# Attention block for 2048 tokens on one core: x transposed on its way from DRAM, constant query rows written by VectorE

## The chip, the cores and the metric

The kernel runs on one core of a Trainium2 chip. The metric is the device time of one execution in microseconds, the median of several runs of the same program.

## What is computed

A whole multi-head attention block in bfloat16, with one batch, S = 2048 tokens, D = 448 features and 16 heads of 28 features:

```python
qkv = (x @ wqkv).reshape(B, S, 3, H, Dh).transpose(2, 0, 3, 1, 4)
q, k, v = qkv[0], qkv[1], qkv[2]
scores = jnp.einsum("bhqd,bhkd->bhqk", q, k) * (Dh ** -0.5)
p = softmax(scores, axis=-1)
o = jnp.einsum("bhqk,bhkd->bhqd", p, v)
return o.transpose(0, 2, 1, 3).reshape(B, S, D) @ wo
```

## The kernel before

**Tiling.** The 16 heads are worked on in four groups of four (G = 4, HG = 4); each head has a slot of 32 partitions, 28 of them features, so that four heads fill 128 partitions. Queries come in four blocks of 512 (NQC), keys in 16 tiles of 128. A "set" is one group with one query block; there are 16 sets. For each set the scores of a key tile against 512 queries are made on TensorE (L730), turned into exponentials by ScalarE (L928, two half steps of 512 in one pass) or by an approximation in integer arithmetic on VectorE (L943, then L1014 or a GpSimd fill at L979 and an accumulating DMA at L990 for its further terms), and multiplied with V into the bank `o` (L1073). Each score carries a bound in place of the row maximum: it is added through extra rows of the query tile `QP`, which stand beside the 28 features of each head. Some of these rows are constant (the value OFFS), one row per query block holds the bound `su`.

**The beginning.** x is loaded by eight DMAs (`load_x`, L138) in four blocks of 512 rows, each as 128 partitions with 4 rows of 448 (row `16 p + t` of x lies on partition `p`, L133), half of them issued by SP and half by ScalarE's queue. After blocks 0 and 1 come the key and query weights of head group 0 (`load_w0`, L142, into `WG`), and behind x, on SP, all weights of V, Q and K (`load_w`, L135, three DMAs). TensorE transposes each block in pieces of 128 rows by 112 columns (`xt_job`, L613: 16 transposes a block at L621), and ScalarE (L629) and VectorE (L627) copy the results to `XT`, so that features lie on 112 partitions in four chunks. While nothing has landed TensorE runs ten matmuls on zeros to warm up (L643).

`k_first` (L376) then makes the keys of group 0 for each block `sc`: 16 matmuls with `WG[1]` (L298, `mm_proj`), a square of the result on ScalarE (L324), an evacuation to `KA` on VectorE (L393) or ScalarE (L390), a matmul with `blockK` that sums the squares (L409) and a maximum over them on VectorE (L414). After the last block the maximum of all four (L418) and a root by bits (L420) follow. `q_job` makes the first query block (`z`, L457), `qn_first` (L484) its norms and the bound: `nq` (L491), then `su` (L496), which needs the maximum over all keys. With `su` there the first scores can be made. `rows_first` (L658) and `place` (L499) bring `z` and `su` into the tile `QP` by DMAs on SP; until they have landed (`wide`, L734) every score is made by two matmuls, one with `z` and one with `su`.

The constant rows of the 16 tiles `QP` are made by 16 VectorE memsets to zero (L194), followed by 16 small DMAs on SP (L198) that bring OFFS into two partitions each. GpSimd fills constants in the meantime: the identity (L166), the clear of V and its column of ones (L209, L210), the output weights (L216, L219).

**What sets the order.** The kernel has no loops at run time and the compiler does not reorder it. A planner in Python (L234 to L1291) keeps a clock for each engine, a list of jobs (`add`) with an assumed duration, the events that each needs (`need`) and gives, the PSUM bank that it takes (`acq`) and a priority (`pri`, the lowest goes first), and emits instructions in the order of that plan. Each engine then runs its own instructions strictly in this order. The landing times of the first loads are assumed (L637): x's blocks at 4.9, 6.2, 8.0 and 9.3 us, group 0's weights at 6.9, the other weights at 10.9 (V), 12.0 (Q) and 13.2 (K). Two rules of the plan matter here: the banks `a0`, `a1`, `d0`, `d1`, `o` and `m` are handed from job to job, and while nothing else is ready, TensorE gets fillers on zeros (`dense`, L758).

Of the kernel before, what the change touches and what calls it, by code (L numbers as in the profile page):

```python
# [39 lines left out]
def kernel(  # L40
# [7 lines left out]
    nc = tc.nc  # L48
# [5 lines left out]
    G = 4  # L54
    HG = 4
    CC = 4
    CK = D // CC
    QW = 512
    NQC = S // QW
    NKT = S // P  # L60
# [35 lines left out]

    x2 = x[0]
    out2 = out[0]
    out_perm = out2.rearrange("(p t) d -> p t d", t=NKT)

    const = ctx.enter_context(tc.tile_pool(name="const", bufs=1))
    big = ctx.enter_context(tc.tile_pool(name="big", bufs=1))
# [1 line left out]
    wk = ctx.enter_context(tc.tile_pool(name="wk", bufs=2))  # L104
    dram = ctx.enter_context(tc.tile_pool(name="dram", bufs=2, space=bass.MemoryType.DRAM))

    XT = [[big.tile([CK, CC // 2, QW], BF16, name=f"XT{b}_{k}") for k in range(2)] for b in range(NXB)]
    WRAW = [big.tile([CK, CC, D + WPAD], BF16, name=f"WRAW{t}") for t in range(3)]
    WG = [wk.tile([P, QW], F32, name=nm, bufs=n)[0:CK, 0:CC * (HG * Dh + WPAD) // 2].bitcast(BF16)
          .rearrange("p (c n) -> p c n", c=CC) for nm, n in (("rr", 1), ("o_sb", 2))]  # L110
# [2 lines left out]
    for k in range(NTERM):  # L113
# [4 lines left out]
        for b in range(NXB):  # L118
# [4 lines left out]
    xs = [big.tile([P, XB, D], BF16, name=f"xs{b}") for b in range(NXB)]  # L123
    QP = [[[big.tile([P, QW], BF16, name=f"QP{c}_{k}_{z}") for z in range(2)] for k in range(2)] for c in range(NQC)]
    OTL = [big.tile([P, QW], BF16, name=f"OTL{c}") for c in range(NQC)]

    def otile(g, c):
        if g < G - 1:
            return xs[c][:].rearrange("p t d -> p (t d)")[:, g * QW:(g + 1) * QW]
        return OTL[c][:]  # L130

    wq3 = wqkv.rearrange("(cc p) n -> p cc n", p=CK)
    x3 = x2.rearrange("(p t) c -> p t c", t=NKT)  # L133

    def load_w(t, eng):  # L135
        eng.dma_start(out=WRAW[t][:, :, 0:D], in_=wq3[:, :, t * D:(t + 1) * D])

    def load_x(b, eng, k=0, n=1):  # L138
        w = XB // n
        eng.dma_start(out=xs[b][:, k * w:(k + 1) * w, :], in_=x3[:, b * XB + k * w:b * XB + (k + 1) * w, :])  # L140

    def load_w0(t, eng):  # L142
        eng.dma_start(out=WG[t], in_=wq3[:, :, t * D:t * D + HG * Dh + WPAD])

    load_x(0, nc.sync, 0, 2)
    load_x(0, nc.scalar, 1, 2)
    for b in range(1, NXB):
        load_x(b, nc.sync, 0, 2)
        load_x(b, nc.scalar, 1, 2)
        if b == 1:  # L150
            load_w0(1, nc.sync)
            load_w0(0, nc.scalar)
    load_w(2, nc.sync)
    load_w(0, nc.sync)
    load_w(1, nc.sync)

    from concourse.hw_specs import get_activation_tables
    for idx, funcs in enumerate(get_activation_tables(nc.m.arch, ()).values()):
# [3 lines left out]
            break  # L162


    ident = const.tile([P, P], BF16, name="ident")
    nc.gpsimd.memset(ident[:], 0.0)  # L166
    nc.gpsimd.affine_select(out=ident[:], in_=ident[:], compare_op=ALU.not_equal,
# [9 lines left out]
    offs = wk.tile([P, 2 * QW], BF16, name="pt", bufs=NPT)[0:2, 0:QW]  # L177
# [4 lines left out]
    for i in range(HG):  # L182
# [4 lines left out]
        nc.vector.memset(blockK[rows, HP * i:HP * (i + 1)], MARG4)  # L187
        for c in range(NQC):
            nc.vector.memset(maskK[rows, c, HP * i + Dh + c:HP * i + Dh + c + 1], 1.0)
    nc.vector.memset(offs, OFFS)  # L190
    for c in range(NQC):
        for k in range(2):
            for z in range(2):
                nc.vector.memset(QP[c][k][z][:], 0.0)  # L194
    for z in range(2):
        for c in range(NQC):
            for k in range(2):
                nc.sync.dma_start(out=QP[c][k][z][HP * k + Dh + NQC - 1 - c:P:2 * HP, :], in_=offs)  # L198
    nc.gpsimd.memset(qoff[:], 0.0)
    for i in range(HG):  # L200
        nc.gpsimd.affine_select(out=qoff[:], in_=qoff[:], compare_op=ALU.not_equal, fill=OFFS,
                                base=-(HP * i + Dh + NQC - 1), pattern=[[0, 1]], channel_multiplier=1)
    for t in range(3):
        nc.gpsimd.memset(WRAW[t][:, :, D:D + WPAD], 0.0)

    def clear_v(g, b):
        v = VT[0][g, b]
# [22 lines left out]
    def bank_tile(tg):  # L230
        return psum.tile([P, QW], F32, name=tg, tag=tg, bufs=1)
# [61 lines left out]
    def mm_proj(ps, t, g, c, ccs):  # L293
        for cc in ccs:
            for i in range(HG):
                h = g * HG + i
                w = WG[t] if g == 0 else WRAW[t]
                nc.tensor.matmul(out=ps[HP * i:HP * (i + 1), :], lhsT=w[:, cc, h * Dh:h * Dh + HP],  # L298
                                 rhs=XT[c][cc // 2][:, cc % 2, :], start=(cc == 0), stop=(cc == CC - 1),
                                 tile_position=(0, HP * i))  # L300
# [240 lines left out]
    def v_job(g, b, t0, bank, pri, gate=0, eng="DVE"):  # L541

        key = ("V", g, b, t0)
        n = XB if g is not None else XB // 2
        parts = n
        g0, g1 = (g, g + 1) if g is not None else (GH, G)
        w = (g1 - g0) * HG * Dh

        def mm(part):
            if part == 0:  # L550
                held[key] = bank_tile(bank)
            for u in range(part * n // parts, (part + 1) * n // parts):
                for cc in range(CC):
                    quarters(held[key][:, u * w:(u + 1) * w], XT[b][cc // 2][:, cc % 2, (t0 + u) * P:(t0 + u + 1) * P],
                             WRAW[2][:, cc, g0 * HG * Dh:g1 * HG * Dh], cc == 0, cc == CC - 1)
# [57 lines left out]
    def xt_job(b, banks, pri):  # L613
        def tr(hf):
            held[("xt", b, hf)] = bank_tile(banks[hf])
            v = held[("xt", b, hf)][:].bitcast(BF16)
            for c2 in range(CC // 2):
                for t in range(XB):
                    k = c2 * XB + t
                    cc = hf * CC // 2 + c2  # L620
                    nc.tensor.transpose(out=v[0:CK, k * P:(k + 1) * P],  # L621
                                        in_=xs[b][:, t, cc * CK:(cc + 1) * CK], identity=ident[:])

        def evac(hf):
            src = held.pop(("xt", b, hf))[:].bitcast(BF16)[0:CK, 0:2 * QW].rearrange("p (c q) -> p c q", c=2)
            if hf == 1:
                nc.vector.tensor_copy(out=XT[b][hf][:], in_=src)  # L627
            else:
                nc.scalar.copy(out=XT[b][hf][:], in_=src)  # L629

        for hf in range(2):
            add("PE", 0.5, lambda hf=hf: tr(hf), need=[("x", b)], gives=[("xt", b, hf)], acq=banks[hf], pri=pri + 0.01 * hf,
                cols=896)
            add("DVE" if hf else "ACT", 0.65 if hf else 0.97, lambda hf=hf: evac(hf), need=[("xt", b, hf)],
                gives=[("XT", b, hf)], rel=banks[hf], pri=pri)

    for n, t in (("x", 0), 4.9), (("G", 1), 6.9), (("G", 0), 6.9), (("x", 1), 6.2), (("x", 2), 8.0), (("x", 3), 9.3), \  # L637
            (("W", 2), 10.9), (("W", 0), 12.0), (("W", 1), 13.2):
        evt[n] = (t, "DMA")

    warm = bank_tile("o")
# [4 lines left out]
    for c in range(NQC):  # L646
        for z in range(2):
            evt[("QZ", c, z)] = (6.5, "DVE")
    for b in range(NXB):
        xt_job(b, ("d0", "d1") if b % 2 == 0 else ("o", "m"), 1.0 * b)  # L650
    k_first(0, "a0", None, "DVE", "ACT", 1.5)
    k_first(1, "a1", "o", "ACT", "ACT", 3.05, late=("ksq", 0, NQC - 1))
    k_first(2, "d0", "a0", "ACT", "ACT", 3.1, late=("ksq", 0, NQC - 1))
    k_first(3, "d1", "o", "DVE", "ACT", 3.2, late=("QA", 0, 0))
    q_job(0, 0, "m", QPRI, split=1)
    qn_first("a0", 3.3)

    def rows_first():  # L658
        for i in range(HG):
            r = slice(HP * i, HP * i + Dh)  # L660
            nc.sync.dma_start(out=QP[0][i % 2][0][r, :], in_=qtt[0][r, :])

    add("SP", 2.4, rows_first, need=[("Q", 0, 0), ("QZ", 0, 0)], gives=["QR00"], land=1.6, pri=0)
    for b in range(NXB):
        v_job(0, b, 0, "m", 7 + 4 * b, eng="ACT" if b == 0 else "DVE")
# [715 lines left out]
```

## Time and profile before

| | |
|---|---|
| median of 3 runs | 361.38 us (361.24 to 361.72) |
| the profiled execution | 361.72 us, its span 359.9 us |
| granted TensorE clock | 0.998 |
| busy, share of the span | PE 95%, ACT 95%, DVE 93%, POOL 47% |
| chain that ended last | PE 37%, ACT 30%, DVE 23%, issue 9%, DMA 1% |
| first exponential of the main loop (L928) | starts at 19.39 us |
| exponentials by ScalarE (L928) | 358, 1129 ns each |
| half steps on VectorE (L943) | 278 from `d`, 30 from `m`, 680 ns each |

PE is TensorE, PEld its weight loads, DVE VectorE, ACT ScalarE, POOL GpSimd and SP the engine that only issues DMAs. Times count from the beginning of the span. The chain of work that ended last goes back from the last instruction: at each step to what released it, or to the instruction before it on its engine. So what stands in it is work without which the end would have been earlier, as far as the trace shows it. Durations are those that the profiler recorded; an instruction can overlap the next of its engine, so two of them may start closer together than one lasts.

### The profile page before, as it was taken

What the parts mean: (1) busy time and instruction counts of PE and PEld (TensorE: products, weight loads), DVE (VectorE), ACT (ScalarE), POOL (GpSimd) and SP (SyncE); (2) the same over time, 40 slices, a digit from 0 to 9 for tenths busy, and PEclk for the clock granted to TensorE, in tenths of its full rate; (3) what the DMA queues carried; (4) which work ended last, traced back from release to release, by engine and by line L of the source; (5) the groups of instructions that cost most, each with busy time, mean ns of one, the idle gap of its engine ahead of it and who ended that gap; (6) DMA issues with size and microseconds to landing.
All of it is one profiled execution on the core that took longest, in us unless ns stands there. A gap on an engine that the chain in (4) does not pass through costs nothing.

```text
span 359.9 us, 11256 instructions
## 1 busy us (share of the span) xinstructions
PE 343.1 (95%) x4520; PEld 111.3 (31%) x4521; DVE 335.4 (93%) x617; ACT 341.1 (95%) x373; POOL 170.2 (47%) x213
## 2 busy tenths in 40 slices
PE   8999999999999999999999999999889999999995
PEld 4533233332234322332232222222222222222233
DVE  8689999999989999999899999999999999999863
ACT  3789999999999999999999999999999999999991
POOL 8951353655444483545635765465546362521010
PEclk9999999999999999999999999999999999999999
DMA  8620063555636765365577646377857685672111
GB/s 242 142 47 15 21 125 86 113 107 105 135 75 129 148 124 113 89 132 108 117 143 149 120 91 137 78 152 158 177 116 156 128 176 129 142 147 66 34 51 54
DMA packets 24017, 41.17 MB, mean 114 GB/s; under 512 B 8604, under 2 KB 15004, under 8 KB 23964
## 3 DMA queue, kind: packets, MB, share of 16 engines
q0 software_dynamic: 8432, 29.24, 42.0%
q1 hardware_dynamic: 14348, 10.07, 10.3%
q10 hardware_dynamic: 1184, 1.14, 1.0%
q8 instruction: 35, 0.57, 0.6%
q14 instruction: 18, 0.15, 0.1%
HBM read 7.58 MB, written 1.96 MB: 27 GB/s over the span
## 4 chain that ended last, share of the span: by engine, by line
PE 37%; ACT 30%; DVE 23%; issue 9%; DMA 1%; DVEq 0%; ACTq 0%
ACT pt L928 30%; PE a L730 12%; DVE I L943 10%; PE o L1073 10%; PE m L305 5%; DVE J L1014 5%; PE m L298 4%; DVE V L579 2%; DVE V L566 2%; DVE KA L338 1%; PE o L643 1%; PE d L730 1%; DVE QA L460 1%; DVE o_sb L1100 1%; PE d L621 1%
## 5 line engine op out<-in xcount | busy, mean ns | idle before, releaser
L928 ACT ACTIVATE pt<-a 128x1024 bf16<-128x1024 f32 x358 | 329.7, 1129 | 2.9 <-PE a L730 1.3
L943 DVE TENSOR_SCALAR I<-d 128x512 int16<-128x512 f32 x278 | 181.0, 680 | 10.1 <-PE d L730 8.8
L730 PE MATMUL a<-QP,KA 32*128 32x512 bf16 (+1 forms) x704 | 137.3, 381 | 8.9 <-ACT pt L928 8.0
L1073 PE MATMUL o<-pt,V 128*32 128x512 bf16 x716 | 105.2, 384 | 0.0
L730 PE MATMUL d<-QP,KA 32*128 32x512 bf16 (+1 forms) x273 | 95.7, 383 | 0.8 <-DVE I L943 0.2
L730 PEld LDWEIGHTS <-KA 32*128 32x128 bf16 (+1 forms) x1041 | 46.1, 91 | 143.5 <-issue 141.7
L990 POOL DMA_DIRECT2D J<-I x55 | 49.6, 902 | 73.0 <-DVE I L943 49.6
L1073 PE MATMUL o<-J,V 128*32 128x512 bf16 x616 | 82.7, 384 | 0.0
L979 POOL MEMSET J<- 128x1024 int32 x55 | 60.1, 1094 | 36.7 <-PE d L730 12.0
L1014 DVE TENSOR_SCALAR J<-I 128x2048 int16<-128x2048 int16 x99 | 73.9, 764 | 0.6
L1073 PE MATMUL o<-I,V 128*32 128x512 bf16 x308 | 64.3, 384 | 0.1
L1073 PEld LDWEIGHTS <-V 128*32 128x32 bf16 x1640 | 30.8, 94 | 48.2 <-issue 45.1
L1123 POOL TENSOR_TENSOR xs<-o_sb,rr 128x512 bf16<-128x512 f32 x12 | 16.9, 1404 | 27.3 <-DVE J L1014 26.9
L298 PE MATMUL m<-XT,WRAW 112*32 112x512 bf16 x384 | 29.6, 384 | 0.2 <-DVE QA L460 0.2
L320 POOL TENSOR_TENSOR sq<-QA 128x512 bf16<-128x512 bf16 x15 | 16.8, 1122 | 23.1 <-DVE QA L460 17.8
L305 PE MATMUL m<-WRAW,XT 112*32 112x112 bf16 (+1 forms) x768 | 20.7, 230 | 0.3 <-DVE KA L338 0.3
L943 DVE TENSOR_SCALAR I<-m 128x512 int16<-128x512 f32 x30 | 20.3, 678 | 0.0
L320 POOL TENSOR_TENSOR sq<-KA 128x512 bf16<-128x512 bf16 x12 | 14.2, 1185 | 9.4 <-DVE J L1014 8.5
L305 PEld LDWEIGHTS <-XT 112*32 112x32 bf16 x768 | 12.3, 96 | 11.5 <-issue 11.4
L305 PE MATMUL m<-WO,xs 128*32 128x448 bf16 x156 | 12.5, 358 | 0.0
L730 PE MATMUL m<-QP,KA 32*128 32x512 bf16 (+1 forms) x30 | 11.5, 384 | 0.0
L460 DVE CAST QA<-m 128x512 bf16<-128x512 f32 x15 | 10.2, 683 | 0.7 <-PE m L298 0.7
(116 smaller groups left out, 207.3 us busy)
## 6 DMA issues: line engine op xcount, KB each, us to landing
J<-I POOLq DMA_DIRECT2D x55, 512.0 KB, 4.9
rr<-scr SPq DMA_DIRECT2D x60, 64.0 KB
QP<-QA SPq DMA_DIRECT2D x60, 28.0 KB
out_dram<-osb SPq DMA_DIRECT2D x12, 112.0 KB
WRAW<-in_wqkv_dram SPq DMA_DIRECT2D x3, 392.0 KB
xs<-in_x_dram ACTq DMA_DIRECT2D x4, 224.0 KB
xs<-in_x_dram SPq DMA_DIRECT2D x4, 224.0 KB
QP<-su SPq DMA_DIRECT2D x32, 2.0 KB
```

The lines of the kernel that those rows point to most:

```text
L298: nc.tensor.matmul(out=ps[HP * i:HP * (i + 1), :], lhsT=w[:, cc, h * Dh:h * Dh + HP], rhs=XT[c][cc // 2][:, cc % 2, :], start=(cc == 0), s ...
L305: nc.tensor.matmul(out=out[r, :], lhsT=lhsT[:, r], rhs=rhs, start=start, stop=stop, tile_position=(0, HP * i), **k)
L320: after_shared(nc.gpsimd.tensor_tensor(out=t[:], in0=src, in1=src, op=ALU.mult))
L460: nc.vector.tensor_copy(out=t[:], in_=held[key][:, 0:QW])
L730: nc.tensor.matmul(out=out_ap, lhsT=KAt[(g, j // XB)][r, (j % XB) * P:(j % XB + 1) * P], rhs=q[r, :], start=(n == 0), stop=(n == len(terms ...
L928: nc.scalar.activation(out=pt[:], in_=ps[:], func=ACT.Exp, scale=LN2 / 128.0)
L943: nc.vector.tensor_scalar(out=dst, in0=pd[:], scalar1=BIAS, scalar2=0.0, op0=ALU.add, op1=ALU.max)
L979: m = nc.gpsimd.memset(ch[1][:].bitcast(I32), fill)
L990: after_shared(nc.gpsimd.dma_start(out=ch[1][:, w], in_=ch["I"][:, w], accum_op=ALU.add))
L1014: cur["shared"] = nc.vector.tensor_scalar(out=r[:, w], in0=ch["I"][:, w], scalar1=float(SHIFT[k]), scalar2=None, op0=ALU.add)
L1073: nc.tensor.matmul(out=o[HP * i:HP * (i + 1), :], lhsT=VT[e["k"]][g, j // XB][:, j % XB, HP * i:HP * (i + 1)], rhs=e["ap"], start=(SETMM[k ...
L1123: m = nc.gpsimd.tensor_tensor(out=otile(g, c), in0=st["o_sb"][:], in1=st["rr"][:], op=ALU.mult)
```

## The change

- x is no longer loaded and transposed on TensorE. Five transposing DMAs, all issued by SP, bring it from DRAM to SBUF with features on partitions, in chunks of 128 columns. The first one brings columns 320 to 447 of all 2048 rows (`XE`), the other four bring columns 0 to 383 of 512 rows each (`XT[b]`). Columns 320 to 383 so lie in two chunks; the weights of the last chunk are zero for them (rows 0 to 63, cleared by VectorE for `WG`, by GpSimd for `WRAW`). `xt_job` with its transposes and copies goes.
- The rows of x lie in their own order, so the output is stored as blocks of 128 rows in a row.
- The weights of group 0 are issued first, by ScalarE's queue, in two DMAs each (384 rows and 64 rows). V's weights follow x's five transfers on SP. The Q and K weights of the other groups become a job of the plan on SP behind the event `QP00`, when the first query rows and bounds are in place.
- The 16 memsets and 16 small DMAs for the constant rows go. GpSimd makes a small table `offs` (128 x 8), and VectorE writes each of the 16 tiles `QP` by one pass that adds a column of `offs` to a tile of zeros.
- Banks and priorities of the first jobs are changed, and so are the assumed landing times: x's blocks at 6.6, 8.1, 9.6 and 11.1 us, group 0's weights at 4.9, V's weights at 13.2.

```diff
-    CK = D // CC
+    CK = P
+    CT = D - CK
...
-    out_perm = out2.rearrange("(p t) d -> p t d", t=NKT)
+    out_perm = out2.rearrange("(t p) d -> p t d", p=P)
...
+    XT = [big.tile([CK, CC - 1, QW], BF16, name=f"XT{b}") for b in range(NXB)]
+    XE = big.tile([CK, 1, S], BF16, name="XE")
...
+    def xt(b, cc):
+        return XT[b][:, cc, :] if cc < CC - 1 else XE[:, 0, b * QW:(b + 1) * QW]
...
-    load_x(0, nc.sync, 0, 2)
-    load_x(0, nc.scalar, 1, 2)
-    for b in range(1, NXB):
-        load_x(b, nc.sync, 0, 2)
-        load_x(b, nc.scalar, 1, 2)
-        if b == 1:
-            load_w0(1, nc.sync)
-            load_w0(0, nc.scalar)
+    def load_w(t, eng, n=D):
+
+        dst = WG[t] if n < D else WRAW[t][:, :, 0:D]
+        cols = slice(t * D, t * D + n)
+        eng.dma_start(out=dst[:, 0:CC - 1, :], in_=wqkv[0:(CC - 1) * CK, cols].rearrange("(cc p) n -> p cc n", p=CK))
+        eng.dma_start(out=dst[CC * CK - D:CK, CC - 1, :], in_=wqkv[(CC - 1) * CK:D, cols])
+
+    def load_x(b):
+        rows = slice(b * QW, (b + 1) * QW)
+        nc.sync.dma_start_transpose(out=XT[b][:], in_=x2[rows, 0:(CC - 1) * CK])
+
+    for t in range(2):
+        nc.vector.memset(WG[t][0:CC * CK - D, CC - 1, :], 0.0)
+    for t in (1, 0):
+        load_w(t, nc.scalar, HG * Dh + WPAD)
+    nc.sync.dma_start_transpose(out=XE[:], in_=x2[:, CT:D])
+    for b in range(NXB):
+        load_x(b)
     load_w(2, nc.sync)
-    load_w(0, nc.sync)
-    load_w(1, nc.sync)
...
+    offs = const.tile([P, 2 * NQC], F32, name="offs")
+    nc.gpsimd.memset(offs[:], 0.0)
+    for k in range(2):
+        for j in range(2):
+            nc.gpsimd.affine_select(out=offs[:, k:2 * NQC:2], in_=offs[:, k:2 * NQC:2], compare_op=ALU.not_equal, fill=OFFS,
+                                    base=-(HP * (k + 2 * j) + Dh + NQC - 1), pattern=[[1, NQC]], channel_multiplier=1)
...
-    nc.vector.memset(offs, OFFS)
-    for c in range(NQC):
-        for k in range(2):
-            for z in range(2):
-                nc.vector.memset(QP[c][k][z][:], 0.0)
     for z in range(2):
         for c in range(NQC):
             for k in range(2):
-                nc.sync.dma_start(out=QP[c][k][z][HP * k + Dh + NQC - 1 - c:P:2 * HP, :], in_=offs)
+                nc.vector.tensor_scalar(out=QP[c][k][z][:], in0=zero[:], scalar1=offs[:, 2 * c + k:2 * c + k + 1], scalar2=None,
+                                        op0=ALU.add)
...
         nc.gpsimd.memset(WRAW[t][:, :, D:D + WPAD], 0.0)
+        nc.gpsimd.memset(WRAW[t][0:CC * CK - D, CC - 1, 0:D], 0.0)
...
-    for n, t in (("x", 0), 4.9), (("G", 1), 6.9), (("G", 0), 6.9), (("x", 1), 6.2), (("x", 2), 8.0), (("x", 3), 9.3), \
-            (("W", 2), 10.9), (("W", 0), 12.0), (("W", 1), 13.2):
+    for n, t in [(("XT", k, h), 6.6 + 1.5 * k) for k in range(NXB) for h in range(2)] + \
+            [(("G", 1), 4.9), (("G", 0), 4.9), (("W", 2), 13.2)]:
         evt[n] = (t, "DMA")
...
-    for b in range(NXB):
-        xt_job(b, ("d0", "d1") if b % 2 == 0 else ("o", "m"), 1.0 * b)
-    k_first(0, "a0", None, "DVE", "ACT", 1.5)
-    k_first(1, "a1", "o", "ACT", "ACT", 3.05, late=("ksq", 0, NQC - 1))
-    k_first(2, "d0", "a0", "ACT", "ACT", 3.1, late=("ksq", 0, NQC - 1))
-    k_first(3, "d1", "o", "DVE", "ACT", 3.2, late=("QA", 0, 0))
+    k_first(0, "a0", "o", "DVE", "ACT", 1.5)
+    k_first(1, "a1", "a0", "ACT", "ACT", 3.05)
+    k_first(2, "d0", "o", "ACT", "ACT", 3.1)
+    k_first(3, "d1", "a0", "DVE", "ACT", 3.2, late=("QA", 0, 0))
     q_job(0, 0, "m", QPRI, split=1)
-    qn_first("a0", 3.3)
+    qn_first("m", 3.15)
...
+    for t in range(2):
+        add("SP", 0.8, lambda t=t: load_w(t, nc.sync), need=["QP00"], gives=[("W", t)], land=6.0, pri=3)
     add("SP", 2.4, rows_first, need=[("Q", 0, 0), ("QZ", 0, 0)], gives=["QR00"], land=1.6, pri=0)
```

In `mm_proj` and in V's projection, `XT[c][cc // 2][:, cc % 2, :]` becomes `xt(c, cc)`.

More of the change, by code (lines that the diff above doesn't have):

```diff
@@ L105 @@
     dram = ctx.enter_context(tc.tile_pool(name="dram", bufs=2, space=bass.MemoryType.DRAM))
-    XT = [[big.tile([CK, CC // 2, QW], BF16, name=f"XT{b}_{k}") for k in range(2)] for b in range(NXB)]
+    XT = [big.tile([CK, CC - 1, QW], BF16, name=f"XT{b}") for b in range(NXB)]
+    XE = big.tile([CK, 1, S], BF16, name="XE")
     WRAW = [big.tile([CK, CC, D + WPAD], BF16, name=f"WRAW{t}") for t in range(3)]
@@ L122 @@
             VT[k][None, b] = t[:]
-    xs = [big.tile([P, XB, D], BF16, name=f"xs{b}") for b in range(NXB)]
+    xs = [big.tile([P, (G - 1) * QW], BF16, name=f"xs{b}") for b in range(NXB)]
     QP = [[[big.tile([P, QW], BF16, name=f"QP{c}_{k}_{z}") for z in range(2)] for k in range(2)] for c in range(NQC)]
     OTL = [big.tile([P, QW], BF16, name=f"OTL{c}") for c in range(NQC)]
+    def xt(b, cc):
+        return XT[b][:, cc, :] if cc < CC - 1 else XE[:, 0, b * QW:(b + 1) * QW]
     def otile(g, c):
         if g < G - 1:
-            return xs[c][:].rearrange("p t d -> p (t d)")[:, g * QW:(g + 1) * QW]
+            return xs[c][:, g * QW:(g + 1) * QW]
         return OTL[c][:]
[L132 to L143, printed above, removed]
-    load_x(0, nc.sync, 0, 2)
-    load_x(0, nc.scalar, 1, 2)
-    for b in range(1, NXB):
-        load_x(b, nc.sync, 0, 2)
-        load_x(b, nc.scalar, 1, 2)
-        if b == 1:
-            load_w0(1, nc.sync)
-            load_w0(0, nc.scalar)
+    def load_w(t, eng, n=D):
[13 more added lines that the diff above has]
+        load_x(b)
     load_w(2, nc.sync)
-    load_w(0, nc.sync)
-    load_w(1, nc.sync)
     from concourse.hw_specs import get_activation_tables
@@ L176 @@
     qoff = const.tile([P, 1], F32, name="qoff")
-    offs = wk.tile([P, 2 * QW], BF16, name="pt", bufs=NPT)[0:2, 0:QW]
     maskK = const.tile([P, NQC, P], BF16, name="maskK")
@@ L298, in mm_proj @@
                 nc.tensor.matmul(out=ps[HP * i:HP * (i + 1), :], lhsT=w[:, cc, h * Dh:h * Dh + HP],
-                                 rhs=XT[c][cc // 2][:, cc % 2, :], start=(cc == 0), stop=(cc == CC - 1),
+                                 rhs=xt(c, cc), start=(cc == 0), stop=(cc == CC - 1),
                                  tile_position=(0, HP * i))
@@ L553, in mm @@
                 for cc in range(CC):
-                    quarters(held[key][:, u * w:(u + 1) * w], XT[b][cc // 2][:, cc % 2, (t0 + u) * P:(t0 + u + 1) * P],
+                    quarters(held[key][:, u * w:(u + 1) * w], xt(b, cc)[:, (t0 + u) * P:(t0 + u + 1) * P],
                              WRAW[2][:, cc, g0 * HG * Dh:g1 * HG * Dh], cc == 0, cc == CC - 1)
@@ L610, in oproj_job @@
         old.append(key + ("st",))
[L613 to L635, printed above, removed]
-    for n, t in (("x", 0), 4.9), (("G", 1), 6.9), (("G", 0), 6.9), (("x", 1), 6.2), (("x", 2), 8.0), (("x", 3), 9.3), \
-            (("W", 2), 10.9), (("W", 0), 12.0), (("W", 1), 13.2):
+    for n, t in [(("XT", k, h), 6.6 + 1.5 * k) for k in range(NXB) for h in range(2)] + \
+            [(("G", 1), 4.9), (("G", 0), 4.9), (("W", 2), 13.2)]:
         evt[n] = (t, "DMA")
```

## The prediction

> **What bounds the kernel now.** I read the chain of work that ended last first, from the start to 30 us. Columns: start us, length us, engine, tile, line, count.
>
> ```profile
> 1.19 4.45 PE o L643 x10
> 5.64 1.49 PE d L621 x16
> 7.13 0.45 PE o L621 x8
> 7.57 0.45 PE m L621 x8
> 8.02 0.98 PE a L298 x16
> 9.00 1.03 PE d L621 x16
> ...
> 11.01 0.58 PE o L621 x8
> ...
> 11.81 0.45 PE m L621 x8
> ...
> 14.85 1.01 PE d L298 x16
> ...
> 15.94 0.70 ACT sq L324
> ...
> 17.10 0.70 DVE kp L414
> ...
> 18.20 0.50 DVE su L496
> ```
>
> Until 15.86 the end hangs on TensorE: ten warming matmuls, then transposes (L621, 1.49+0.45+0.45+1.03+0.58+0.45 = 4.45 us of chain) between projections (L298). After the last key projection (issued at 14.78 by the timeline) comes a chain of hand-offs: square, norm, maximum, root, bound `su`, ended at 18.69. The first exponential starts at 19.39. So from that projection's issue to `su` takes 3.91 us, and to the first exponential 4.61 us.
>
> The table by stretches of time shows the rest (PE, PEld, DVE, ACT, POOL busy; clock; DMA share; GB/s):
>
> ```profile
> 3.00:6.00 3.00, 3.00 (x13) 1.39 (x12) 2.98 (x12) 1.01 (x1) 2.74 (x10) 1.00 1.12 343
> 6.00:9.00 3.00, 3.00 (x46) 2.29 (x45) 2.54 (x7) 2.30 (x3) 2.77 (x9) 1.00 1.07 331
> ```
>
> ```profile
> 19.39:320.00 300.61, 290.03 (x3827) 89.82 (x3829) 290.50 (x495) 298.42 (x325) 149.24 (x159) 1.00 0.57 117
> ```
>
> In the early stretches the DMA engines are full; from 19.39 to 320 ScalarE works 298.42 of 300.61 us. That stage has no slack for this change to win or lose much: what the change does to the start of the main loop is passed on to the end. The question is therefore **when the first exponential starts**.
>
> **The change, part by part.** *Removed:* 64 transposes on TensorE (4.45 us of chain), four ScalarE copies of 1.008 us and four VectorE copies of 0.67 to 0.69 us. What is late next is the data. Before, x and the first weights (2.04 MB) moved from 2.00 us (first packet) to 9.20 us (last packet of x), 283 GB/s, and the last key projection still waited for transposes and copies until 14.78.
>
> *Added: the transposing transfers.* Overlapping columns make them 0.52 MB (one, 2048 rows of 256 B) and 4 x 0.39 MB (rows of 768 B): 2.10 MB, with 0.21 MB of first weights beside them. No row shows a transposing transfer. By the packet records, a 232 B packet holds an engine for 18 ns, so sixteen engines make 206 GB/s; 1792 B takes 74 ns (387 GB/s); 64 B takes 11.8 ns (87 GB/s). The reads have runs nearest to the first two rows, so I take 206 GB/s for the 256 B runs and for the weights, and the whole load's 283 GB/s for the 768 B runs: 2.55 + 1.01 + 5.56 = 9.1 us. From 2.00 that lands the last block at about 11.2. Bounds: all at 387 GB/s, 8.0; all in 64 B pieces, 2.00 + 24.2 + 1.0 = 27.2.
>
> *The sum.* The key projection of block 3 then starts at 11.35 in place of 14.78: 3.43 us earlier. TensorE has room: from block 0's landing (2.00 + 2.55 + 1.01 + 1.39, about 7.0) to 11.35 it needs four projections of 0.98 (three key blocks and the query, which has the same inputs as block 0) and a few norms of 0.32 each. Its warming matmuls end at 5.64, and fillers stand in the plan after them.
>
> *Constant rows.* VectorE loses sixteen memsets of 0.272 us (4.4) and gains sixteen tensor_scalar passes. The nearest row is L579 (128x512 bf16 to bf16, 0.274 to 0.289 us); the one pass with a pointer scalar and SBUF source, L496, took 0.488. So 4.5 to 7.8 us from about 2.55: done at 7.0 to 10.4. I take 7.0, by L579, which has the types. Before the last maximum (about 13.7), VectorE still owes one evacuation, three maxima, `z` and `nq`, 3.96 us by their starts in the timeline; so passes that end by 9.7 cost nothing, those at 10.4 cost 0.7. Without this cover every us is paid (rival 1).
>
> *SP.* The sixteen `QP<-pt` issues held SP until 19.14, so `QP<-z` (ready at 16.3) was issued from 19.24 to 22.46 and `QP<-su` from 22.56; the first score matmuls on `QP` came at 25.14. Until then each score round is done twice (`z`, then `su`): six rounds, 0.21 us extra each, on a TensorE that carries the chain from 18.7 to 25.9. Now SP is free after the five transposes and W2's two issues, `QP<-z` goes out while the keys are worked on, and the two `QP<-su` follow `su`. By the same 2.6 us from there, the doubled stretch shrinks from 6.4 to 2.6 us. That is 3.5 rounds, 0.7 us; I take half, 0.4, as V projections fill the same stretch (ends 0 and 0.7). W0 and W1, four issues of about 0.45 us, move behind this; their first reader stood at 44.67, 20 us of cover. W2 is queued behind the last transpose: 0.40 MB in 62 ns packets of 896 B, 1.7 us, lands at about 12.9; V's projection, in line behind block 3's norm at 13.4, hides it by 0.5.
>
> *GpSimd.* Five small operations for `offs` (0.25 each) and three memsets of 64x448 (0.46 each by L209): 2.6 us. Its first square followed 7.07 us of idling, which hides it. The stores change only their address.
>
> Sum: 3.4 + 0.4 = 3.8 us off the profiled execution's 361.72 (span 359.9): **357.9**. That execution lies 0.34 above the median 361.38, so I predict 357.6 for the median. If 0 and 0.7 are taken for SP and 8.0 for the landing, with work, not data, then in the way for about half of it, the low end is 356.2.
>
> **The rivals.**
>
> *1. VectorE and GpSimd shut each other out.* The timeline of 63.6 to 66.5:
>
> ```profile
> 63.59 1.27 POOL L979 MEMSET J<- 128x1024 int32 x1
> 64.35 2.07 DVE L1014 TENSOR_SCALAR J<-I 128x2048 int16<-128x2048 int16 x1
> 64.51 1.35 POOL L320 TENSOR_TENSOR sq<-KA 128x512 bf16<-128x512 bf16 x1
> ```
>
> The VectorE pass (median 0.685) took 2.07: it ended 0.56 after the second GpSimd operation, which was issued after it and ran first. All sixteen new passes are of that kind, and GpSimd fills and clears almost without a break from 0.7 to 14. The memsets they replace never waited (0.272 min and max). If passes and GpSimd instructions alternate, sixteen pairs of 0.28 + 0.33 end at about 12.4; if one pass fits in per fill-and-clear pair (0.65 to 1.14), at about 19. VectorE then owes 5.5 us to `su`, with key norms queued behind it on PSUM banks: the point of decision is about 12.3, the time 361 in the first case and, with `su` at 25, 367.5 in the second. Against it: passes issued back to back may hold VectorE's turn, and GpSimd leaves 0.06 us gaps. Chance 0.21, 0.18 of it slower. The Trainium skill, "SBUF — State Buffer", section "Who interferes with whom", states the rule that speaks against this change: tensor_scalar in a two-port mode and a GpSimd instruction exclude each other for a whole instruction, and the one issued first wins. The rows agree on the exclusion, but above the later issued one ran first.
>
> *2. Transposing is slower than the reads.* It decides at a landing of 14.65, where block 3 is no earlier than before: 2.31 MB in 12.65 us, 182 GB/s. If the blocks are written in small pieces, the 64 B row gives a landing at 27.2, 12.6 us late: 374. With 32 B pieces (between 4 B, 9 ns, and 64 B) at 10.5 ns it is 46 us, 392. For it: no row shows such a transfer, and packets below 232 B are poor. Against it: nothing shows that the small pieces cost packets of their own. Chance 0.22. Worse still, one engine could carry it block by block: 32 KB at 74 ns per 1792 B is 1.35 us, and 64 blocks end at 89 us: 435. Chance 0.03. The skill has both sides: "VectorE: DVE Perf Modes", section "The three transpose paths", gives 1309 ns for a 128x128 block by DMA against 390 on TensorE, which for 64 blocks one after another is an estimate of 84 us; "DMA: Bandwidth & Descriptors", section "Latency and other measured facts", gives 261 GB/s for transposes, an estimate of 8.0 us for 2.10 MB. No run here shows either.
>
> *3. The early start is given back.* The order of all engines is planned from assumed landing times; another split of exponentials between ScalarE and VectorE, or W2 landing behind its plan and holding TensorE ahead of the first scores, costs the 3 us: 361. Chance 0.07, mostly no change.
>
> **How the numbers follow.** The forecast has 0.47, all faster. Rival 1 adds 0.03 to no change and 0.18 to slower, rival 2 0.25 to slower, rival 3 0.05 and 0.02. That gives faster 0.47, same 0.08, slower 0.45; 0.2% (0.7 us) is about what a measurement of this kernel can tell from no change. Forecast and losses are nearly even, so the range must reach far up: to 374, the 64 B price, leaving out half of rival 2 (0.13) and about 0.04 below 356.2. The forecast's own range is 356.2 to 360.
>
> **What would show it.** Right: x's transfers landed by about 11.2, block 3's key projection at 11.4, the sixteen passes near 0.28 us each and ended by 9.7, `su` near 15.3, the first exponential near 16, and a main loop as long as before. Rival 1: passes of 0.8 us or more beside GpSimd memsets. Rival 2: key projections that wait for DMA past 14.65, with TensorE idle or on fillers. Wrong altogether: a first exponential before 17 and no gain at the end.

## The result and the profile after

The changed kernel takes 366.62 us (median; 365.83 to 367.16) beside 361.55 us for the kernel before: 1.0129 times as long, 95% interval 1.0093 to 1.0165. It is slower by about 5 us where 3.8 us less were forecast.

| from the profiled execution | before | after |
|---|---|---|
| span | 359.9 us | 364.6 us |
| last key projection of group 0 issued | 14.78 | 17.37 |
| first exponential of the main loop | 19.39 | 23.42 |
| from there to the end of the span | 340.5 | 341.2 |
| exponentials on ScalarE, half steps on VectorE | 358, 308 | 360, 304 |
| granted TensorE clock | 0.998 | 0.991 |

So 4.0 of the 4.7 us stand before the first exponential. The chain of work that ended last in the changed kernel, from 2 to 24 us (start, length, engine, tile, line, count):

```profile
2.42 2.94 DVE QP L198 x5
5.36 0.55 issue
5.91 4.16 DVE QP L198 x7
10.06 1.01 issue
11.08 4.29 DVE QP L198 x4
15.37 0.71 DVE KA L395
16.08 0.73 DVE z L459
...
16.86 0.59 PE m L489
17.44 1.83 PE d L300 x12
...
21.13 0.70 DVE kp L416
...
22.23 0.50 DVE su L498
```

In place of TensorE's transposes the sixteen VectorE passes at L198 now carry the chain from 2.42 to 15.37. Only then come the evacuation of block 0's keys (L395) and of the queries (L459), which stood behind the passes in VectorE's queue; the squares on ScalarE that come before them (L326) had ended at 9.15 and 10.01. TensorE, in its fixed order, waits for them with block 3's projection (L300), whose data had been complete since 13.0.

The passes by themselves (count: shortest, median, longest ns, then first and last start):

```profile
L198 DVE TENSOR_SCALAR QP<-zero,offs x16: 348/758/2098, 2.4 to 14.6; 128x512 bf16<-128x512 bf16 x16
```

The timeline of VectorE and GpSimd from 3.2 us, other engines left out; the first line merges two passes (the fourth and the fifth):

```profile
3.21 2.77 DVE L198 TENSOR_SCALAR QP<-zero,offs 128x512 bf16<-128x512 bf16 x2
3.32 0.46 POOL L206 MEMSET WRAW<- 64x448 bf16 x1
...
3.73 0.10 POOL L205 MEMSET WRAW<- 128x16 bf16 x1
...
3.78 0.46 POOL L206 MEMSET WRAW<- 64x448 bf16 x1
...
4.18 0.10 POOL L205 MEMSET WRAW<- 128x16 bf16 x1
...
4.23 0.46 POOL L206 MEMSET WRAW<- 64x448 bf16 x1
...
4.64 0.52 POOL L211 MEMSET V<- 128x512 bf16 x1
...
5.22 0.20 POOL L212 MEMSET V<- 128x16 bf16 x1
```

The first three passes started 0.26 us apart and took 0.35 each. The fourth started at 3.21. GpSimd's clears of `WRAW` began after it, at 3.28, and followed each other without a gap; that pass took 2.10 us. After the first 128x512 clear of V (4.64 to 5.16) GpSimd left 0.06 us, and one pass got in; from there one pass per pair of fills, 0.75 us each, and 1.25 each beside the clears of 128x1024.

The table by stretches of time (PE, PEld, DVE, ACT, POOL busy; clock; DMA share; GB/s):

```profile
12.00:15.00 3.00, 0.47 (x12) 0.00 (x0) 3.00 (x4) 1.36 (x2) 2.83 (x7) 0.82 0.59 153
15.00:18.00 3.00, 1.75 (x10) 0.43 (x14) 3.00 (x6) 0.00 (x0) 3.00 (x7) 0.50 0.05 12
18.00:21.00 3.00, 2.94 (x16) 0.54 (x8) 1.29 (x2) 0.69 (x1) 3.00 (x7) 0.54 0.34 77
```

While TensorE waited, the granted clock fell to 0.50. The last projection and the norms behind it ran at that clock (the twelve matmuls at 17.37 took 1.47 us, those at 11.43, at full clock, 0.83): from its issue to the first exponential 6.05 us went by, 4.61 before.

The packet records of the trace show the transfers. All 2.10 MB moved as 8192 packets of 256 B, the 768 B rows too; a packet held an engine for 18 ns in the median and 20.6 in the mean. The last packets of the parts ended at about 4.8 (`XE`), 6.7, 8.1, 10.2 and 12.4 us. But an engine that waits for a transfer is released by its completion, which the trace shows as semaphore updates, and the last of these came later: 5.9 (`XE`), 7.3, 9.3, 11.4 and 13.0 us. The projection of block 2 shows it, with a wait that ends at 11.43 and not at 10.2:

```profile
11.43 0.83 PE L300 MATMUL d<-XT,o_sb 128*32 128x512 bf16 x12 [0.73 <-DMA XT<-in_x_dram]
```

### The profile page after: what moved, and what is told of

It is laid out like the page before. It is cut to its first block, busy times and chain, and to the rows that moved or that the text cites. A ratio compares the mean times of both kernels' runs of the same rounds, so it can differ in the third digit from the quotient of the medians.

```text
span 364.6 us, 11051 instructions
## 1 busy us (share of the span) xinstructions
PE 338.7 (93%) x4438; PEld 108.2 (30%) x4438; DVE 335.5 (92%) x609; ACT 338.9 (93%) x371; POOL 171.6 (47%) x219
## 4 chain that ended last, share of the span: by engine, by line
ACT 38%; PE 35%; DVE 17%; issue 8%; POOL 1%; DVEq 0%; ACTq 0%
ACT pt L905 38%; PE a L707 13%; PE o L1050 11%; DVE I L920 5%; PE m L307 4%; PE m L300 4%; DVE QP L198 3%; DVE J L991 3%; DVE QA L462 1%; DVE V L581 1%; DVE KA L340 1%; PE d L707 1%; PE d L300 1%; PE m L739 0%; PE d L307 0%
## 5 line engine op out<-in xcount | busy, mean ns | idle before, releaser
L920 DVE TENSOR_SCALAR I<-d 128x512 int16<-128x512 f32 x271 | 177.1, 680 | 15.0 <-PE d L707 13.4
L707 PE MATMUL d<-QP,KA 32*128 32x512 bf16 (+1 forms) x268 | 92.7, 383 | 0.1
L1050 PE MATMUL o<-J,V 128*32 128x512 bf16 x608 | 79.3, 384 | 0.0
L991 DVE TENSOR_SCALAR J<-I 128x2048 int16<-128x2048 int16 x98 | 70.2, 732 | 0.4
L300 PE MATMUL m<-XT,WRAW 128*32 128x512 bf16 x288 | 24.4, 386 | 0.3
L920 DVE TENSOR_SCALAR I<-m 128x512 int16<-128x512 f32 x33 | 22.4, 679 | 0.2 <-PE m L707 0.2
L322 POOL TENSOR_TENSOR sq<-KA 128x512 bf16<-128x512 bf16 x12 | 13.3, 1141 | 10.5 <-DVE KA L340 5.5
L307 PE MATMUL m<-WRAW,XT 128*32 128x112 bf16 (+1 forms) x576 | 17.6, 231 | 0.0
L198 DVE TENSOR_SCALAR QP<-zero,offs 128x512 bf16<-128x512 bf16 x16 | 13.0, 884 | 0.0
L307 PEld LDWEIGHTS <-XT 128*32 128x32 bf16 x576 | 9.4, 95 | 10.1 <-issue 9.9
```

Of the source, the lines that this page charges most:

```text
L198: nc.vector.tensor_scalar(out=QP[c][k][z][:], in0=zero[:], scalar1=offs[:, 2 * c + k:2 * c + k + 1], scalar2=None, op0=ALU.add)
L322: after_shared(nc.gpsimd.tensor_tensor(out=t[:], in0=src, in1=src, op=ALU.mult))
L707: nc.tensor.matmul(out=out_ap, lhsT=KAt[(g, j // XB)][r, (j % XB) * P:(j % XB + 1) * P], rhs=q[r, :], start=(n == 0), stop=(n == len(terms ...
L920: nc.vector.tensor_scalar(out=dst, in0=pd[:], scalar1=BIAS, scalar2=0.0, op0=ALU.add, op1=ALU.max)
L991: cur["shared"] = nc.vector.tensor_scalar(out=r[:, w], in0=ch["I"][:, w], scalar1=float(SHIFT[k]), scalar2=None, op0=ALU.add)
L1050: nc.tensor.matmul(out=o[HP * i:HP * (i + 1), :], lhsT=VT[e["k"]][g, j // XB][:, j % XB, HP * i:HP * (i + 1)], rhs=e["ap"], start=(SETMM[k ...
```

## The experiments

Times are medians; "loop" is the time from the first exponential to the end of the span in the profiled execution. Each ratio is to executions of the kernel before at the same time, with medians of 361.40 us (e1 to e4), 361.66 (e5 to e8) and 361.55 (after, e9, e10).

| kernel | time | ratio to before, 95% interval | first exponential | loop |
|---|---|---|---|---|
| before | 361.55 | | 19.39 | 340.5 |
| after | 366.62 | 1.0129 (1.0093 to 1.0165) | 23.42 | 341.2 |
| e1, clears wait | 362.07 | 1.0024 (1.0007 to 1.0041) | 17.68 | 342.3 |
| e2, single chunks | 368.88 | 1.0207 (1.0187 to 1.0227) | 25.40 | 341.4 |
| e3, before with passes | 369.99 | 1.0237 (1.0217 to 1.0256) | 27.33 | 340.3 |
| e4, rows on GpSimd | 379.12 | 1.0489 (1.0470 to 1.0508) | 19.14 | 358.9 |
| e5, e1 with other due times | 361.73 | 1.0001 (0.9990 to 1.0012) | 18.68 | 341.5 |
| e6, e1 with GpSimd planned at 24 | 361.31 | 0.9995 (0.9981 to 1.0008) | 17.54 | 341.2 |
| e7, before with GpSimd planned at 30 | 367.15 | 1.0154 (1.0141 to 1.0168) | 19.02 | 346.3 |
| e8, e3 with waiting clears | 361.47 | 1.0002 (0.9991 to 1.0013) | 19.21 | 342.1 |
| e9, e6 with two blocks | 364.96 | 1.0095 (1.0078 to 1.0111) | 21.57 | 342.6 |
| e10, after with GpSimd planned at 24 | 367.27 | 1.0155 (1.0139 to 1.0170) | 23.63 | 341.9 |

**e1: is it the port?** GpSimd's clears wait for the last pass; nothing else changes.

```diff
-                nc.vector.tensor_scalar(out=QP[c][k][z][:], in0=zero[:],
+                lastp = nc.vector.tensor_scalar(out=QP[c][k][z][:], in0=zero[:],
...
-        nc.gpsimd.memset(WRAW[t][:, :, D:D + WPAD], 0.0)
+        mw = nc.gpsimd.memset(WRAW[t][:, :, D:D + WPAD], 0.0)
+        if t == 0:
+            tc.add_manual_dep(mw.ins, lastp.ins.name, ...)
```

> The changed kernel, but GpSimd's first clear of WRAW (and so all its clears behind it) waits until VectorE's last constant-row pass is done. Same instructions, same work. Theory A (port): a pass of VectorE and an instruction of GpSimd exclude each other, and GpSimd's run of clears held the passes up. Then the sixteen passes follow each other every 0.26 us, as the first three did, end near 6.9 us in place of 15.4, the last key projection starts when the data has landed (12.7) in place of 17.37, the first exponential comes near 17.4 in place of 23.42, and the time is near 366.6 - 6.0 = 360.6 us. Theory B (the passes are slow beside the transposing transfers that write to SBUF, or slow of themselves): passes stay near 0.8 us, the time stays at 366 to 367. Theory C (the start does not matter, the loop that follows got slower): first exponential at 17.4 and still 365 or more.

The passes in e1:

```profile
L198 DVE TENSOR_SCALAR QP<-zero,offs x16: 348/348/353, 2.4 to 6.4; 128x512 bf16<-128x512 bf16 x16
```

They are the same instructions, beside the same transposing transfers: 0.348 us each, ended at 6.7 in place of 15.4. Theory B falls: it was GpSimd's clears that held the passes up. Three lines of e1's timeline show what followed:

```profile
13.07 0.83 PE L303 MATMUL d<-XT,o_sb 128*32 128x512 bf16 x12
...
16.49 0.49 DVE L501 TENSOR_SCALAR su<-V,kroot 128x512 bf16<-128x512 f32 x1
...
17.68 1.02 ACT L908 ACTIVATE pt<-a 128x1024 bf16<-128x1024 f32 x1 [0.76 <-PE a L710]
```

The projection of block 3 starts at 13.07, the first exponential at 17.68, exactly the 4.61 us later that stood between them before, at a clock of 1.00. The start is 5.7 us earlier than after the change and 1.7 earlier than before it. Yet the time, 362.07, is 1.5 us above what theory A gave, and 0.24% above the kernel before, mostly since the loop grew from 340.5 to 342.3.

A part of this is the same collision, come back later. With the wait GpSimd's clears last until 19.9, in the kernel before they were over at 13.9, and there they meet VectorE's next passes of the same kind (tensor_scalar, 128x512 bf16), the two of `V<-V`:

```profile
16.69 1.32 POOL L214 MEMSET V<- 128x1024 bf16 x1
...
17.62 2.48 DVE L584 TENSOR_SCALAR V<-V 128x512 bf16<-128x512 bf16 x2
...
18.12 1.82 POOL L221 MEMSET WO<- 128x448 bf16 x4
```

In the kernel before, with the clears long over, the two took 0.49:

```profile
19.33 0.49 DVE L579 TENSOR_SCALAR V<-V 128x512 bf16<-128x512 bf16 x2
```

The 2.48 us stand in e1's chain of work that ended last. VectorE's half steps come behind them, the banks of their scores come free late, and ScalarE waits 0.73 us before its fifth exponential, which starts 4.79 us after the first, against 4.09 in the changed kernel with the same numbers of passes and half steps. That is 0.7 of the 1.1 us by which e1's loop is longer than the changed kernel's (341.2).

**e3 and e8: the passes without the transposing transfers.** e3 is the kernel before with the table `offs` and the sixteen passes; e8 adds the wait of e1.

```diff
-                nc.vector.memset(QP[c][k][z][:], 0.0)
...
-                nc.sync.dma_start(out=QP[c][k][z][HP * k + Dh + NQC - 1 - c:P:2 * HP, :], in_=offs)
+                nc.vector.tensor_scalar(out=QP[c][k][z][:], in0=zero[:], scalar1=offs[:, 2 * c + k:2 * c + k + 1], ...)
```

> The kernel before with one part of the change alone: the sixteen memsets and sixteen small DMAs for the constant rows replaced by the table of GpSimd and the sixteen passes of VectorE; no transposing transfer anywhere. Theory A: GpSimd's clears hold the passes up here too; they end near 14 to 15 us, VectorE's copies of x stand behind them, so the first key projection starts near 16 in place of 7.95 and the time rises by 6 to 9 us, to 367 to 370. Theory B (slow only beside transposing transfers): passes end near 7 us, the time is 361.5 or, because SP is free earlier, 0.5 us less.

Two lines of e3's timeline:

```profile
2.27 11.28 DVE L198 TENSOR_SCALAR QP<-zero,offs 128x512 bf16<-128x512 bf16 x16
...
14.20 1.04 PE L299 MATMUL a<-XT,o_sb 112*32 112x512 bf16 x8 [6.08 <-DVE XT L628]
```

The passes again end only at 13.55, TensorE waits 6.08 us for VectorE's copy of x that stands behind them, and the kernel loses 8.6 us, more than the whole change. This one part is enough for a loss of that size.

> The kernel before with the constant rows by VectorE's passes, and GpSimd's clears waiting for the last pass. Theory A (port): passes end near 6.8 us, no later than the sixteen memsets before, the first exponential is back from 27.3 to 19.4 and the time at 361.4; since the plan is the same and TensorE's order fixed, SP being free of sixteen small transfers brings nothing, 361.0 to 361.7. If passes cost in other ways than through GpSimd, some of the 8.6 us stay.

With the wait the passes take 0.344 us each, 4.3 in all, the first exponential is back at 19.21, and the time is that of the kernel before (1.0002). Without GpSimd's clears beside them, no cost of the passes can be seen here, and SP rid of sixteen small transfers brings nothing that can be measured.

**e4: the other way out.** Two passes stay on VectorE, fourteen go to GpSimd behind its clears.

```diff
+    for k in range(2):
+        const_rows(nc.vector, 0, k, 0)
...
+    for z in range(2):
+        for c in range(NQC):
+            for k in range(2):
+                if c or z:
+                    const_rows(nc.gpsimd, c, k, z)
```

> The changed kernel, but only the two passes for the first set's tiles stay on VectorE; the other fourteen run on GpSimd behind its clears of V (the nearest GpSimd rows are 0.46 us for a memset of 64x448 and 1.04 us for a 128x512 tensor_tensor, so 6 to 15 us there, ended by 21 to 29; the next tiles are wanted near 30). Theory A: two passes are done by 3.3 us, before GpSimd's run of clears begins at 3.5, VectorE is free at once, first exponential near 17.4, time near 360.6, with GpSimd's jobs of the main loop later by what exceeds its slack of some 7 us. Theory B and C: as for the kernel with waiting clears (B here gives most of the gain too, as 14 passes are gone from VectorE).

VectorE was free at once. The first exponential came at 19.14, 1.7 us later than expected: block 3's projection waited for its data until 14.08, and the pass for `su` took 0.95 us beside a GpSimd pass, 0.49 in the kernel before. Then the chain of work shows what I had not priced:

```profile
17.49 20.56 POOL QP L196 x12
38.05 1.65 POOL WO L223 x4
```

A pass costs 1.71 us on GpSimd, fourteen end at 38, and the output weights' transfers and the first square come behind them, at 48.5 in place of 30.1; ScalarE and VectorE do nothing from 40 to 50. The loop grew by 18 us. The expected 6 to 15 us for the passes was too low.

**e2 and e9: what sets the pace of the transposing transfers?** e2 is e1 with three transfers of one chunk for each block; e9 is e6 with two transfers of 1024 rows in place of four of 512.

```diff
-        nc.sync.dma_start_transpose(out=XT[b][:], in_=x2[rows, 0:(CC - 1) * CK])
+        for cc in range(CC - 1):
+            nc.sync.dma_start_transpose(out=XT[b][:, cc:cc + 1, :], in_=x2[rows, cc * CK:(cc + 1) * CK])
```

```diff
-        rows = slice(b * QW, (b + 1) * QW)
+        rows = slice(2 * b * QW, 2 * (b + 1) * QW)
...
-    for b in range(NXB):
+    for b in range(NXB // 2):
         load_x(b)
```

> The kernel with waiting clears, and each block of x transposed by three transfers of one chunk of 128 columns in place of one transfer of three chunks: 13 transposing transfers in place of five, the same 8192 packets of 256 B. Theory E (the DMA engines set the pace, 18 to 20 ns a packet): blocks land at the same times as before, the last near 12.6 us, time equal to that of the kernel with waiting clears within 0.5 us. Theory S (SP's issuing of three-chunk transfers sets the pace, 1.5 to 2.4 us each; the one-chunk transfer of 2048 rows took 1.35 us for a third more data): the last block lands near 10.5 to 11 us and the time falls by 1.5 to 2 us. If each transfer has a fixed cost of half a microsecond or more that nothing hides, the last block lands later than 14 and the time rises by 1.5 us or more.

Three lines of e2's timeline:

```profile
0.74 1.34 SPq L153 DMA_TRANSPOSE XE<-in_x_dram  x1
...
2.14 16.12 SPq L147 DMA_TRANSPOSE XT<-in_x_dram  x12
...
17.04 0.62 PE L304 MATMUL d<-XT,o_sb 128*32 128x512 bf16 x4 [1.02 <-DMA XT<-in_x_dram]
```

A transfer of one chunk held SP for 1.34 us with 2048 rows and hardly less, 1.26, with 512 (eleven of the twelve). Thirteen of them issue too slowly: the blocks were complete at 9.3, 12.1, 17.0 and 19.8 us, in e1 at 7.6, 9.5, 11.5 and 13.0. The last of the three outcomes came true, and the time rose by 6.8 us against e1.

> The kernel with waiting clears and GpSimd planned free at 24.0, its four transposing transfers of 512 rows joined to two of 1024 rows; the same 8192 packets of 256 B. Theory E (the engines set the pace: 18 to 20 ns a packet on sixteen engines, 2.0 us for 1536 packets): the last rows land again at 12.3 to 12.8 us, the first exponential stays near 17.7 and the time at 361.0 to 361.6. Theory S (each transfer has a cost of its own on SP or in the queue, since a transfer of 512 rows in one chunk took SP as long, 1.34 us, as one of 2048 rows): two transfers less land the last rows 1 to 2 us earlier, at 10.7 to 11.7, first exponential 16.2 to 16.8, time 359.8 to 360.6.

In e9 SP issues for 8.84 us in place of 8.06 in e1, and the last part was complete at 13.04 us against 13.03 in e1 and 12.76 in e6. Fewer transfers do not move the landing: at four transfers the packets on the sixteen engines set the pace (8192 x 20.6 ns / 16 = 10.5 us; they took 10.06 in the changed kernel). The time rose all the same, by 3.65 us against e6. The table by stretches of e9 says why:

```profile
9.00:12.00 3.00, 2.18 (x24) 0.97 (x27) 0.00 (x0) 0.24 (x1) 2.71 (x10) 0.50 1.15 218
12.00:15.00 3.00, 3.00 (x32) 1.01 (x24) 1.55 (x2) 1.14 (x2) 2.83 (x8) 0.50 0.66 164
```

With blocks 0 and 1 complete together, at 9.78, TensorE had nothing for 3.3 us, and the clock fell to 0.50 until 15; the first three projections, 0.83 us for twelve matmuls in e1, took 1.47 to 1.52. So the first exponential came at 21.57, although the last data was there as early as in e1.

**e5, e6, e7 and e10: the early start given back?** Each changes numbers of the plan alone: e5 the assumed landing times, in e1; e6, e7 and e10 the time from which GpSimd counts as free, in e1, in the kernel before and in the changed kernel. (e5's new times for x, 6.9 to 12.8, are near the ends of the packets; what TensorE waits for came at 7.6 to 13.0 in e1, and in e5 itself the last block was complete only at 13.62.)

```diff
-    for n, t in [(("XT", k, h), 6.6 + 1.5 * k) for k in range(NXB) for h in range(2)] + \
-            [(("G", 1), 4.9), (("G", 0), 4.9), (("W", 2), 13.2)]:
+    for n, t in [(("XT", k, h), (6.9, 8.6, 10.6, 12.8)[k]) for k in range(NXB) for h in range(2)] + \
+            [(("G", 1), 4.9), (("G", 0), 4.9), (("W", 2), 14.6)]:
```

```diff
-    free = {"PE": 0.0, "ACT": 0.0, "DVE": 0.0, "SP": 0.0, "POOL": 26.0}
+    free = {"PE": 0.0, "ACT": 0.0, "DVE": 0.0, "SP": 0.0, "POOL": 24.0}
```

> The kernel with waiting clears, its plan given the landing times that its trace showed (x's blocks 6.9, 8.6, 10.6, 12.8; V's weights 14.6). The plan then splits the half steps as the kernel before does: 358 passes of exponentials on ScalarE and 308 half steps on VectorE, where the changed kernel and the one with waiting clears have 360 and 304. Theory D (the early start is given back by the split): two passes less on a ScalarE that is busy all the time are 2 x 0.926 us, so about 362.1 - 1.9 = 360.2 us, 1.2 us under the kernel before; first exponential again near 17.7. Theory F (the loop is longer for another reason of the change: 128 rows of x in place of 112, the stores, weights that land late): 361.5 to 362.5.

> The kernel with waiting clears, one number of the plan changed that says nothing of x: GpSimd counts as free from 24.0 in place of 26.0. The plan then has 358 passes and 308 half steps too, with the assumed landing times of the change kept. Theory D: about 360.2 us as well, the plan's split alone decides. Theory F: 361.5 to 362.5. If only corrected landing times help, this one stays at 362 and the other one falls.

> The control: the kernel before, nothing of the change in it, but GpSimd counts as free from 30.0 in place of 26.0 in its plan, which there gives 360 passes on ScalarE and 304 half steps on VectorE. Theory D: the time rises by about 1.9 us, to 363.2. Theory F: it stays at 361.4 within 0.5.

> The changed kernel as it is, without waiting clears, but with GpSimd planned free at 24.0 (358 passes on ScalarE and 308 half steps on VectorE, as the kernel before has). If the loss is the late start (first exponential 23.4, 4.0 us after that of the kernel before) plus a plan that costs 0.5 to 1 us more in the loop, the start stays at 23.4 and the time falls by 0 to 1 us, to 365.6 to 366.6, and stays 4 to 5 us above the kernel before. If the plan were the main cause, the time would come down to 363 or less.

Theory D, that two ScalarE passes more cost 2 x 0.926 us, fails as a measure. e5 and e6 came out at 361.73 and 361.31, not 360.2, and the control e7 lost 5.5 us, not 1.9: its profile has 360 passes, and nine times two of them start over 1.33 us apart, where the kernel before has this twice. Theory F gave the times of e5 and nearly of e6, but not that of e7, which has nothing of the change and lost more than the change did. What stays is that the plan's order alone moves the loop by up to 5.8 us, in a way that the number of passes does not tell. For the loss of the changed kernel it is not the cause: e10, with the split of the kernel before, starts at 23.63 and is as slow (367.27).

e6 starts 1.85 us earlier than the kernel before and its profiled execution is 1.2 us shorter (span 358.7 against 359.9), but the median gains 0.35 us only and the interval holds 1. Its executions lie between 360.5 and 363.3, those of the kernel before, at the same time, between 361.1 and 362.2, and the profiled one is the fastest of e6, so its loop says little of the others. In e5 and e6 too the late clears meet VectorE's passes: the two of `V<-V` took 1.49 and 1.24 us, and `su` 0.83 and 0.62 in place of 0.49; but ScalarE shows no wait behind `V<-V` there. One wait inside the loop is seen in e10, from 262 to 267.5:

```profile
POOL xs L1100 <- DMA rr<-scr: 2.8, 1, 2.8
```

GpSimd waits 2.8 us for the transfer `rr<-scr`, VectorE's next pass is late by it, and ScalarE stands for 1.4. The profile of the kernel before has 0.5 us of this wait between 240 and 290; that of e6 has one of 3.0 us, and is e6's fastest execution all the same. So this wait is not shown to make the spread, and why the transfer lands late there I have not tested.

## Why the prediction was wrong

- **What bounds the kernel** held for the loss: ScalarE is busy all through the loop, and the first exponential's delay of 4.0 us arrived at the end. A gain at the start did not arrive in this way: 1.7 us in e1 became a loss of 0.7 in the median, 1.85 in e6 a gain of 0.35.
- **Constant rows: the step that failed.** I priced the sixteen passes at 0.28 us by L579 and let them end at 7.0, against the row in rival 1 that showed a pass of 2.07. The range 0.274 to 0.289 also left out one of L579's own sixteen passes of this form, the first of the two here: it took 0.884, beside a GpSimd memset of the kernel before:

```profile
69.33 1.27 POOL L979 MEMSET J<- 128x1024 int32 x1
...
69.87 1.08 DVE L579 TENSOR_SCALAR V<-V 128x512 bf16<-128x512 bf16 x2
```

A pass takes 0.35 and starts 0.26 after the one before while GpSimd's clears are held back (e1, e8); beside the run of clears it takes 0.75 to 2.10. They ended at 15.4, far past the 12.3 from which I had said it decides. e1, e3 and e8 show that the clears beside the passes are the cause of the late start: take the overlap away and it is gone, with the same instructions. That a shared port is the reason is not shown by these runs; they only agree with it.
- **Rival 1, with 0.21, is what happened**, and its reading of the row was right: the later GpSimd instruction runs first. Its two prices (passes ended at 12.4 or 19, 361 or 367.5 us) stand around the truth: one pass for each pair of fills, 15.4, since the first three passes got through before the clears began. The argument against it, that passes issued back to back hold their turn, failed at the fourth pass. The rule of the Trainium skill ("SBUF — State Buffer", "Who interferes with whom") was right on the exclusion; that the one issued first wins, this trace does not bear out: seven GpSimd instructions issued after the fourth pass ran before it.
- **The transposing transfers** were mis-sized by 1.8 us. I gave the 768 B rows the whole load's 283 GB/s; they moved as 256 B packets, and their last one ended at 12.4 in place of 11.2. The other 0.6 us stand between the last packet and the completion at 13.0, for which I had nothing in the sum. In e1, where nothing else was in the way, every key projection started 0.04 us after its block was complete (the last 13.07 after 13.03). The price that I used for the first transfer, 206 GB/s from the 232 B packets, fits all of them (2.10 MB in 10.06 us, 209 GB/s). Rival 2 did not come about: 13.0 is before the 14.65 from which it decides. The Trainium skill's "DMA: Bandwidth & Descriptors", "Latency and other measured facts", gives 261 GB/s for a non-contiguous case; the measured 209 decides here. The Trainium skill's 1309 ns for a block of 128x128 ("VectorE: DVE Perf Modes", "The three transpose paths") is no price for a bulk transfer: 64 blocks took 10.06 us, 0.16 each.
- **TensorE's clock** I had left out. In the changed kernel, where TensorE waited for VectorE, it cost 1.4 us more (6.05 in place of 4.61 from the last projection to the first exponential, at a clock of 0.50 to 0.54 until 21); e9 shows the same after 3.3 us without work.
- **SP, the doubled scores:** the doubled stretch went from 6.4 to 4.3 us, not to 2.6. e8 and the loop times show no gain that could be told from other differences.
- **GpSimd's 2.6 us more** were hidden in the changed kernel. In e1, with the clears another 3.4 us later, GpSimd's work was not: its last clears met `V<-V`.
- **The early start given back, rival 3,** is true of e1: with the passes out of the way the start gains 1.7 us and the loop takes 1.8 more, 0.7 of it by the collision with `V<-V`. In e6 it gains 1.85, and 0.35 is left in the median. So even with the passes out of the way the forecast of 3.8 us would have failed: the last projection starts 1.7 us later than in the sum (13.07 for 11.35), by the data alone, and the loop takes most of the rest.

What stays open: why the loop after the change is 0.7 us longer (1.0 by the medians), and what e6's loop loses in most of its executions. The plan's order and waits like that for `rr<-scr` may have a part in it; that is not shown. A changed kernel in which the late clears meet neither the sixteen passes nor `V<-V` was not run.

## What to carry to other kernels

Before moving set-up work onto VectorE, look at what GpSimd does in those microseconds: a VectorE tensor_scalar pass from SBUF to SBUF waited for GpSimd's fills here (0.75 to 2.10 us in place of 0.35), and a run of fills without gaps kept out a pass that had started earlier, while a plain memset on VectorE was not held up (L194: 0.272 us each beside GpSimd's clears). If the work must go there, order it with one dependency (GpSimd's fills behind the passes: 4.5 us here), and then look at which passes the delayed fills meet next (`V<-V`, 2.48 us in place of 0.49). And when a row of the profile shows the collision, price it in the forecast and not only in a rival.

## What the runs showed of the hardware that I had not expected

- A run of GpSimd memsets keeps a waiting VectorE pass out until it leaves a gap: 0.06 us after a 128x512 fill was enough for one pass, none came between the 64x448 clears.
- A tensor_scalar pass with a pointer scalar, 128x512 bf16, takes 0.35 us on VectorE (0.26 from start to start) and 1.71 on GpSimd (twelve in 20.56).
- A transposing transfer of one 128-column chunk held SP for 1.34 us with 2048 rows and 1.26 with 512 (e2); one of three chunks with 512 rows 1.5 to 2.4.
- The last completion of a transposing transfer came some 0.6 to 1.2 us after its last packet (13.0 against 12.4 and 11.4 against 10.2 in the changed kernel).
- Rows of 768 contiguous bytes moved in packets of 256 B when they were transposed (8192 packets for 2.10 MB).
